# An attention block with bilinear feed-forward on one core: batch 0's keys in float32 on both hardware queues, and the small units of batches 1 to 4 in new slots

## The chip, the cores and the metric

The kernel runs on one core of a Trainium2 chip. The metric is the device time of one execution in microseconds (us). The core has the matrix engine TensorE (PE in the profile; PEld is its loading of the stationary operand), VectorE (DVE), ScalarE (ACT), GpSimd (POOL) and SyncE (SP). Each runs its own instructions in program order and waits for the others through semaphores. Sixteen DMA engines move data between memory (HBM) and the on-chip buffers. Loads can be issued from SyncE and ScalarE (two hardware queues, q1 and q10 in the profile) and from GpSimd (the software queue, q0). In this kernel only the software queue's loads change the type, from float32 to float16.

## What is computed

```python
# q, k, v: (8, 8, 576, 64)   phi: (8, 8, 576, 32)   float32
a = exp(phi - max(phi)); a = a / sum(a)             # over the 32 memories
k_m = einsum('bhsm,bhsd->bhmd', a, k)               # 32 memory keys per head
v_m = einsum('bhsm,bhsd->bhmd', a, v)
scores = matmul(q, k_m.T) / sqrt(64)
attn = softmax(scores)                              # over the 32 memories
attn_out = matmul(attn, v_m)
x = attn_out as (4608 tokens, 512)
out = ((x @ w_a) * (x @ w_b)) @ w_out               # 512 -> 1536 -> 512, float32 out
```

The kernel works batch by batch (0 to 7). It folds v_m into w_a and w_b (vab), so that the two up projections act on the attention weights A directly; their product is kept in ht, and the down projection multiplies ht by w_out.

## The kernel before: the parts that matter here

Every engine's order is the order in which the Python code emits instructions. A schedule in strings says in which order the small units of each batch are emitted and between which up and down matmuls they stand.

Start of the program (cuts marked):

```python
    def load_phi(b):
        phis[b] = inp.tile([P, NHP, NI * M], F32, name="phi_sb")
        (nc.sync if b == 0 else nc.gpsimd).dma_start(out=phis[b], in_=rows(phi, b))
    ...
    ht = consts.tile([P, NFF, 2 * S], F16, name="ht")
    k_f32 = ht[:, 0:2].bitcast(F32)                 # unused at this time, so a float32 landing place
    nc.scalar.dma_start(out=k_f32, in_=rows(k, 0)[:, 0:2])
    nc.scalar.preload_act_table_set("natural_log_exp_and_others")
    load_phi(0)
    halves = [slice(0, 2), slice(2, 4)]
    load_q(0, halves[0])                            # these four on the software queue
    load_k(0, halves[1])
    load_q(0, halves[1])
    load_v(0)
    ...
    nc.vector.memset(kv_sbs[0][:, 2], 1.0 / CS)
    nc.vector.tensor_copy(out=kvs[0][:, 0, 0:2], in_=k_f32)     # float32 to float16
    load_wab(0, 512)
    ...                                             # ones, then the other weights and batch 1
```

The units named in the schedule (g is one half of the heads):

```
exp0 exp1   ScalarE: exponential of phi, per half of the heads
ks0 ks1     TensorE: sums of a*k and of a, 36 matmuls; VectorE: reciprocal and scaling (kvm)
kt0 kt1     TensorE: transposes of kvm; VectorE: copy to kvT
vs, vt      the same for the values; from batch 2 on kv + km + kvt do both together
qt0..qt3    VectorE: 32x32 transposes of q
s0 s1, sc   TensorE: scores (per half; both halves)
e0 e1       ScalarE: exponential of the scores (E)
den0 den1   TensorE: denominators; ScalarE: logarithm (L)
nr0 nr1     ScalarE: R = exp(-L); A = E*R on VectorE (batches 0, 1) or GpSimd (from batch 2)
v0a, x0a .. TensorE: folds of values into weights; ScalarE and VectorE: copy to vab
aN bN       TensorE: up matmuls; ScalarE copies the first, VectorE multiplies into ht
yN          N matmuls of the first four down blocks
fN          N dummy matmuls (the warm tile)
L           loads of a later batch on the software queue
```

The schedule (cut to the strings concerned):

```python
    fill(16)
    chain(0, "exp0 exp1 qt0 qt1 f12 ks0 f4 kt0 f2 ks1 f1 s0 e0 kt1 qt2 qt3 f2 den0 f4 s1 e1 nr0 f8 vs0 vs1 den1 f2 vt0 vt1 nr1 f4")
    chain(0, "v0a x0a f4 a0 a1 v0b x0b f4 b0 b1 ...")
    ...
    chain(1, "exp0 exp1 y9 ks0 y3 kt0 qt0 qt1 y1 y3 ks1 qt2 s0 e0 y6 kt1 qt3 den0 y3 s1 nr0 e1 y4 y2 den1 vs0 vs1 vt0 y1 vt1 nr1 hv0a hx0a hv0b y3 hx0b y2")
    ...
    ups(half_steps(1, 1, 4), slots(2, "- kvt qt3 sc+e0+e1 - den0+den1 nr0+nr1 v0+x0a x0b - v1+x1b x1a"))
    second = "v2_+x2a_+exp0 x2b_ exp1 - kv+km qt0 qt1 kvt qt2+qt3 sc+e0 e1+v0+x0a ..."
```

A slot of the last two strings stands after one pair of up matmuls, and an apostrophe means the batch after. Partial products of the down projection are pulled in between at an even rate, and their sums of tokens (h_sums) run on GpSimd.

Of the kernel before, what the change touches and what calls it, by code (L numbers as in the profile page):

```python
# [8 lines left out]
F32 = mybir.dt.float32  # L9
# [9 lines left out]
def kernel(  # L19
# [11 lines left out]
    nc = tc.nc  # L31
# [38 lines left out]
    def rows(x, b):  # L70
        return x[b].rearrange("h s d -> (h s d)").rearrange("(c p f) -> p c f", c=NHP, p=P)

    phis, qs, kvs = {}, {}, {}
    kv_sbs = [consts.tile([P, 3, NHP, NI * D], F16, name=f"kv_sb{t}") for t in range(2)]

    def load_phi(b):
        phis[b] = inp.tile([P, NHP, NI * M], F32, name="phi_sb")
        (nc.sync if b == 0 else nc.gpsimd).dma_start(out=phis[b], in_=rows(phi, b))

    def load_k(b, hps=slice(0, NHP)):  # L80
        kvs[b] = kv_sbs[b % 2]
        nc.gpsimd.dma_start(out=kvs[b][:, 0, hps], in_=rows(k, b)[:, hps])

    def load_v(b, hps=slice(0, NHP)):
        nc.gpsimd.dma_start(out=kvs[b][:, 1, hps], in_=rows(v, b)[:, hps])

    def load_q(b, hps=slice(0, NHP)):
        if b not in qs:
            qs[b] = inp.tile([P, NHP, NI * D], F16, name="q_sb")
        nc.gpsimd.dma_start(out=qs[b][:, hps], in_=rows(q, b)[:, hps])  # L90

    def load(b):
        load_phi(b)
        load_k(b)
        load_v(b)
        load_q(b)

    def load_wab(lo, hi):
        nc.gpsimd.dma_start(out=wa_sb[:, :, lo:hi], in_=wa_rows[:, :, lo:hi])
        nc.gpsimd.dma_start(out=wb_sb[:, :, lo:hi], in_=wb_rows[:, :, lo:hi])  # L100
# [4 lines left out]


    ht = consts.tile([P, NFF, 2 * S], F16, name="ht")
    k_f32 = ht[:, 0:2].bitcast(F32)
    nc.scalar.dma_start(out=k_f32, in_=rows(k, 0)[:, 0:2])
    nc.scalar.preload_act_table_set("natural_log_exp_and_others")  # L110
    load_phi(0)
    halves = [slice(0, 2), slice(2, 4)]
    load_q(0, halves[0])
    load_k(0, halves[1])
    load_q(0, halves[1])
    load_v(0)
    kvs[0] = kv_sbs[0]

    warm = consts.tile([P, 512], F16, name="warm")
    nc.vector.memset(warm, 0.0)  # L120
# [26 lines left out]
    def fill(n, cols=512):  # L147

        pw = banks.tile([P, 512], F32, name="pw")
        for _ in range(n):  # L150
            nc.tensor.matmul(pw[:, :cols], warm[:, :P], warm[:, :cols], start=True, stop=True)
# [1 line left out]
    ident = consts.tile([P, P], F16, name="ident")  # L153
    make_identity(nc, ident)
    nc.vector.memset(kv_sbs[0][:, 2], 1.0 / CS)
    nc.vector.tensor_copy(out=kvs[0][:, 0, 0:2], in_=k_f32)
    load_wab(0, 512)

    ones = consts.tile([P, 4, 32], F16, name="ones")
# [6 lines left out]
    load_wab(1024, 1536)  # L166
    load_wo(0)
    load_phi(1)
    load_k(1)
    load_q(1, halves[0])  # L170
# [418 lines left out]
    def up_half(b, i, hf, x):  # L589
        ps = banks.tile([P, HALF], F32, name=("pa", "pb")[x])  # L590
        for g in range(2):
            nc.tensor.matmul(ps, vabs[b][x][:, g, P * i:P * (i + 1)], attn[b][:, g, HALF * hf:HALF * (hf + 1)],  # L592
                             start=(g == 0), stop=(g == 1))
        if x == 0:
            if b == 0:
                n = (2 * i + hf) % 20
                a_sbs[b, i, hf] = spare[:, HALF * n:HALF * (n + 1)]
            else:
                a_sbs[b, i, hf] = apool.tile([P, HALF], F16, name="a_sb")
            nc.scalar.copy(out=a_sbs[b, i, hf], in_=ps)  # L600
        else:
            t0 = S * (b % 2) + HALF * hf
            nc.vector.tensor_tensor(out=ht[:, i, t0:t0 + HALF], in0=a_sbs.pop((b, i, hf)), in1=ps, op=ALU.mult)  # L603

    def up(b, i, hfs):
        for hf in hfs:
            up_half(b, i, hf, 0)
        if len(hfs) > 1:
            yield
        for hf in hfs:  # L610
            up_half(b, i, hf, 1)
        yield

    def ups(steps, side=()):

        side = iter(side)
        for step in steps:
            for _ in up(*step):
                work.advance()
                next(side, us[step[0]]["-"])()  # L620
        for f in side:
            work.advance()
            f()
# [5 lines left out]
    def half_steps(b, hf, lo=0):  # L629

        return [(b, i, (hf,)) for i in range(lo, NFF)]
# [10 lines left out]
    def slots(b, names):  # L642

        def both(fs):
            return lambda: [f() for f in fs]
        def unit(n):
            if n == "fin":
                return lambda: work.pull(-work.done % NFF)
            if n == "L":
                return lambda: load(b + 2) if b + 2 < B else None  # L650
            if n[0] == "y":
                return lambda: some(int(n[1:]))
            if n[0] == "d" and n[1:].isdigit():
                return lambda: work.pull(int(n[1:]))
            return us[b + n.endswith("'") - n.endswith("_")][n.rstrip("'_")]

        return [both([unit(n) for n in x.split("+")]) for x in names.split()]
# [3 lines left out]
    def some(n):  # L661
        for _ in range(n):
            next(early, None)

    def chain(b, plan):


        for x in plan.split():
            if x[0] == "f":
                fill(int(x[1:]), 256)  # L670
            elif x[0] == "y":
                some(int(x[1:]))
            elif x[0] in "ab":
                i, _, hf = x[1:].partition(".")
                for h in ([int(hf)] if hf else (0, 1)):
                    up_half(b, int(i), h, "ab".index(x[0]))
            else:
                us[b][x]()
# [3 lines left out]
    chain(0, "v0a x0a f4 a0 a1 v0b x0b f4 b0 b1 a2 b2 v1a x1a a3 b3 a4 a5 v1b x1b a6 a7 b4 b5 v2a x2a b6 b7 a8 a9")  # L682
    load(2)
    chain(0, "v2b x2b a10 a11 b8 b9 b10 b11")
    chain(1, "exp0 exp1 y9 ks0 y3 kt0 qt0 qt1 y1 y3 ks1 qt2 s0 e0 y6 kt1 qt3 den0 y3 s1 nr0 e1 y4 y2 den1 vs0 vs1 vt0 y1 vt1 nr1 hv0a hx0a hv0b y3 hx0b y2")
    load(3)
    sum_weights()
    ups(steps(1, 0, 4), slots(1, "- hv1a+hx1a hv1b+hx1b+y1 - v1a+x1a y3+v1b x1b y3"))
    ups(half_steps(1, 0, 4), slots(1, "- v2a+x2a+v2b+x2b+qt0' - - qt1'+exp0'+qt2' exp1' - kv'+km'+y9"))
    work.plan(S + HALF, 10)  # L690
    ups(half_steps(1, 1, 4), slots(2, "- kvt qt3 sc+e0+e1 - den0+den1 nr0+nr1 v0+x0a x0b - v1+x1b x1a"))
    second = "v2_+x2a_+exp0 x2b_ exp1 - kv+km qt0 qt1 kvt qt2+qt3 sc+e0 e1+v0+x0a den0+x0b v1+x1a nr0+L x1b+exp0' den1 - nr1+v2+x2a - x2b+exp1' - kv'+km' qt0'+qt1' - qt2'+kvt'+qt3'"
    every = "- sc+e0 e1 den0 v0+x0a+x0b - - nr0+exp0' - - v1+x1a qt0' x1b+den1 exp1' - v2+x2a+x2b nr1+qt1' kv'+km' qt2' - qt3' - kvt'+L -"
    last = "sc+e0 - e1 - v0+x0b - x0a den1 - - den0 v1+x1b x1a+nr0 - - - - nr1+v2+x2a - - - - - x2b"
    for b in range(2, B):
# [37 lines left out]
```

The softmax here doesn't subtract the row's maximum and nothing guards it: scores larger than these inputs give would overflow.

## Time and profile before

| what | value |
|---|---|
| median of 3 runs | 245.89 us (245.75 to 246.15) |
| profiled span | 244.0 us, granted TensorE clock 0.996 |
| busy: TensorE, VectorE, ScalarE, GpSimd | 234.6, 166.2, 157.2, 155.6 us |
| read from HBM, written | 42.47 MB, 9.44 MB |
| TensorE busy from 0 to 8 us, 8 to 16, 16 to 24 | 6.74, 6.93, 7.41 us |
| from 32 to 41, 41 to 49, 63 to 74 | 8.05, 7.68, 10.36 us |
| from 230 to 244 | 9.83 us |
| to landing: phi and first keys of batch 0 (hardware queues) | 6.2 and 5.8 us |
| to landing: second keys of batch 0 (software queue) | 7.6 us |

The page's second part cuts the span into 40 slices of 6.1 us, and each digit is the busy share of a slice in tenths. A line of the time line reads: start in us, duration in us, engine, line of the program, operation, output and input tiles, shape, number of instructions merged, and in brackets how long the engine stood idle before and what ended the wait. A line of the waits reads: engine, tile and line, whom it waited for, total us, times, longest. Where several matmuls are merged, the duration runs from the first start to the last end, so that a wait between them is inside it; the end of a matmul is modelled, and those of neighbours overlap.

### The profile page before, as it was taken

How to read it: one execution, taken by the hardware profiler on the slowest of the kernel's cores; microseconds unless marked ns; L12 is line 12 of the kernel's file. 1: busy time of each engine (PE TensorE's matmuls, PEld its weight loads, DVE VectorE, ACT ScalarE, POOL GpSimd, SP SyncE). 2: the span in 40 equal slices, each digit the busy share in tenths (PEclk: the TensorE clock that was granted, in tenths of full speed). 3: DMA queues.
4: the chain of work that ended last, by engine and by line, in shares of the span. 5: the costliest groups of instructions: out<-in, count | busy, mean ns of one | idle time of the engine just before them, and what ended most of it. 6: DMA issues, size and time to landing. Idle time of an engine off the chain costs nothing.

```text
span 244.0 us, 7661 instructions
## 1 busy us (share of the span) xinstructions
PE 234.6 (96%) x3043; PEld 168.1 (69%) x3043; DVE 166.2 (68%) x401; ACT 157.2 (64%) x406; POOL 155.6 (64%) x130
## 2 busy tenths in 40 slices
PE   7989998999989999999999999999999999999993
PEld 2555654456757857767788777877787878888882
DVE  3446773568949968875994659865996676756642
ACT  2265761679598589578956768587856867565330
POOL 8722263499879629892889759892849177937001
PEclk9999999999999999999999999999999999999998
DMA  6999999999937955973159732696120403042154
GB/s 198 211 207 206 209 254 208 254 224 280 224 89 167 205 110 121 236 128 81 41 146 205 177 86 46 166 203 152 34 58 3 89 0 87 3 89 61 42 128 118
DMA packets 25044, 33.82 MB, mean 139 GB/s; under 512 B 1936, under 2 KB 19472, under 8 KB 25008
## 3 DMA queue, kind: packets, MB, share of 16 engines
q0 software_dynamic: 18288, 22.84, 50.8%
q1 hardware_dynamic: 6208, 9.70, 15.8%
q10 hardware_dynamic: 512, 0.79, 1.0%
q8 instruction: 24, 0.39, 0.7%
q14 instruction: 12, 0.10, 0.1%
HBM read 42.47 MB, written 9.44 MB: 213 GB/s over the span
## 4 chain that ended last, share of the span: by engine, by line
PE 76%; DMA 16%; DVE 3%; ACT 2%; issue 1%; POOL 0%; DVEq 0%
PE pa L592 17%; PE py L464 17%; PE pb L592 16%; PE pv L464 8%; DMA wo_sb<-in_moe_w_out_dram 7%; DMA wa_sb<-in_moe_w_a_dram 6%; PE pva L337 5%; PE px L464 4%; PE po L389 3%; DMA ht<-in_k_dram 2%; PE pkv L212 2%; PE pscore L292 1%; PE pD L314 1%; PE pT L241 1%; ACT E L305 1%
## 5 line engine op out<-in xcount | busy, mean ns | idle before, releaser
L603 DVE TENSOR_TENSOR ht<-a_sb,pb 128x288 f16<-128x288 f16 x168 | 73.2, 448 | 39.4 <-ACT a_sb L600 29.9
L592 PEld LDWEIGHTS <-vab 128*128 128x128 f16 x768 | 71.6, 98 | 27.1 <-issue 9.4
L600 ACT CAST a_sb<-pa 128x288 f16<-128x288 f32 x168 | 66.6, 407 | 26.4 <-PE pa L592 24.3
L592 PE MATMUL pa<-A,vab 128*128 128x288 f16 x384 | 75.7, 287 | 0.4 <-DVE vab L349 0.2
L592 PE MATMUL pb<-A,vab 128*128 128x288 f16 x384 | 75.0, 286 | 0.3 <-ACT vab L349 0.3
L446 POOL TENSOR_TENSOR h_sums<-ht 128x768 f16<-128x768 f16 x28 | 45.9, 1642 | 33.0 <-DVE ht L603 32.4
L464 PEld LDWEIGHTS <-h_sums 128*128 128x128 f16 x384 | 37.3, 98 | 7.0 <-issue 0.5
L349 DVE CAST vab<-pva 128x512 f16<-128x512 f32 (+1 forms) x50 | 32.3, 663 | 3.3 <-PE pva L337 2.6
L349 ACT CAST vab<-pva 128x512 f16<-128x512 f32 (+1 forms) x50 | 27.9, 581 | 9.3 <-PE pva L337 9.1
L464 PEld LDWEIGHTS <-ht 128*128 128x128 f16 x288 | 28.1, 98 | 5.7 <-issue 0.4
L464 PE MATMUL py<-w_sums,h_sums 128*128 128x256 f16 x192 | 30.4, 272 | 0.0
L446 POOL TENSOR_TENSOR h_sums<-ht,h_sums 128x768 f16<-128x768 f16 x14 | 23.0, 1642 | 1.0
L446 POOL TENSOR_TENSOR h_sums<-h_sums,ht 128x768 f16<-128x768 f16 x14 | 23.0, 1642 | 0.9
L325 POOL TENSOR_TENSOR A<-E,R 128x576 f16<-128x576 f16 x12 | 15.3, 1278 | 8.8 <-ACT R L323 8.6
L305 ACT ACTIVATE E<-pscore 128x288 f16<-128x288 f32 x32 | 11.4, 417 | 14.5 <-PE pscore L292 14.5
L464 PE MATMUL pv<-w_sums,h_sums 128*128 128x256 f16 x96 | 16.2, 273 | 0.0
L464 PE MATMUL py<-wo_sb,ht 128*128 128x256 f16 x96 | 16.0, 273 | 0.0
L471 ACT ACTIVATE u<-py 128x256 f32<-128x256 f32 x32 | 12.6, 393 | 5.2 <-PE py L464 4.9
L203 DVE STREAM_TRANSPOSE qT<-q_sb 128x288 f32<-128x288 f32 x32 | 14.3, 461 | 2.3 <-DMA q_sb<-in_q_dram 2.3
L464 PE MATMUL py<-w_sums,ht 128*128 128x256 f16 x96 | 15.5, 272 | 0.1
L464 PE MATMUL px<-wo_sb,ht 128*128 128x256 f16 x96 | 15.4, 273 | 0.0
L194 ACT ACTIVATE exp_sb<-phi_sb 128x576 f16<-128x576 f32 x16 | 11.0, 698 | 5.3 <-DMA phi_sb<-in_phi_dram 5.3
(65 smaller groups left out, 274.5 us busy)
## 6 DMA issues: line engine op xcount, KB each, us to landing
out_dram<-o_sb SPq DMA_DIRECT2D x68, 128.0 KB, 2.4
kv_sb<-in_v_dram POOLq DMA_DIRECT2D x7, 576.0 KB, 11.4
phi_sb<-in_phi_dram POOLq DMA_DIRECT2D x7, 576.0 KB, 5.2
kv_sb<-in_k_dram POOLq DMA_DIRECT2D x7, 576.0 KB, 9.0
q_sb<-in_q_dram POOLq DMA_DIRECT2D x6, 576.0 KB, 13.6
wa_sb<-in_moe_w_a_dram POOLq DMA_DIRECT2D x3, 512.0 KB, 14.4
wb_sb<-in_moe_w_b_dram POOLq DMA_DIRECT2D x3, 512.0 KB, 16.2
wo_sb<-in_moe_w_out_dram POOLq DMA_DIRECT2D x3, 512.0 KB, 18.1
```

The lines of the kernel that those rows point to most:

```text
L194: nc.scalar.activation(out=t["exp"][:, 2 * z:2 * z + 2, :, :], in_=phis[b][:, 2 * z:2 * z + 2, :].rearrange("p c (i m) -> p c i m", m=M), ...
L203: nc.vector.transpose(out=t["qT"][:, hp, :].bitcast(F32), in_=qs[b][:, hp, :].bitcast(F32))
L305: nc.scalar.activation(out=Ev[:, g, :, z, :], in_=pss, func=AF.Exp, scale=1.0 / (8.0 * CS))
L325: engine.tensor_tensor(out=attn[b][:, g, sl], in0=t["E"][:, g, sl], in1=t["R", g][:, sl], op=ALU.mult)
L337: nc.tensor.matmul(t["pva", lo, z][g][0][32 * j:32 * j + 32, 0:hi - lo], t["kvT"][64 * r:64 * r + 64, 4 + g, M * j:M * j + M], w_sbs[z][64 ...
L349: engine_copy(out=vabs[b][z][:, g, lo:hi], in_=pva[:, 0:hi - lo])
L446: engine.tensor_tensor(out=out, in0=in0, in1=in1, op=op)
L464: nc.tensor.matmul(po, lhs[:, i], rhs[:, i], start=first and i == 0, stop=i == KH - 1, skip_group_check=not first)
L471: nc.scalar.mul(out=x, in_=po, mul=scale)
L592: nc.tensor.matmul(ps, vabs[b][x][:, g, P * i:P * (i + 1)], attn[b][:, g, HALF * hf:HALF * (hf + 1)], start=(g == 0), stop=(g == 1))
L600: nc.scalar.copy(out=a_sbs[b, i, hf], in_=ps)
L603: nc.vector.tensor_tensor(out=ht[:, i, t0:t0 + HALF], in0=a_sbs.pop((b, i, hf)), in1=ps, op=ALU.mult)
```

## The change

Batch 0's keys arrive in two halves of two head pairs each, both in float32, one on each hardware queue, into space of ht that is free until the first up products; VectorE casts each half. phi of batch 0 goes to the software queue ahead of q and the values. This is to have all of the keys early. The order of the small units of batch 1 and of batches 2 to 4 is new in three strings, to have the inputs of a matmul ready when TensorE comes to it.

The diff without what only moves lines:

```diff
-        (nc.sync if b == 0 else nc.gpsimd).dma_start(out=phis[b], in_=rows(phi, b))
+        nc.gpsimd.dma_start(out=phis[b], in_=rows(phi, b))
 ...
-    k_f32 = ht[:, 0:2].bitcast(F32)
-    nc.scalar.dma_start(out=k_f32, in_=rows(k, 0)[:, 0:2])
+    k_f32 = ht[:, 0:4].bitcast(F32)
+    halves = [slice(0, 2), slice(2, 4)]
+    for engine, x in zip((nc.sync, nc.scalar), halves):
+        engine.dma_start(out=k_f32[:, x], in_=rows(k, 0)[:, x])
     nc.scalar.preload_act_table_set("natural_log_exp_and_others")
     load_phi(0)
-    load_q(0, halves[0])
-    load_k(0, halves[1])
-    load_q(0, halves[1])
+    for x in halves:
+        load_q(0, x)
     load_v(0)
 ...
-    nc.vector.tensor_copy(out=kvs[0][:, 0, 0:2], in_=k_f32)
+    for x in halves:
+        nc.vector.tensor_copy(out=kvs[0][:, 0, x], in_=k_f32[:, x])
 ...
-    chain(1, "exp0 exp1 y9 ks0 y3 kt0 qt0 qt1 y1 y3 ks1 qt2 s0 e0 y6 kt1 qt3 den0 y3 s1 nr0 e1 y4 y2 den1 vs0 vs1 vt0 y1 vt1 nr1 hv0a hx0a hv0b y3 hx0b y2")
+    chain(1, "exp0 y1 exp1 y11 ks0 ks1 y1 qt0 y3 kt0 qt1 s0 e0 kt1 y6 qt2 qt3 den0 y3 s1 nr0 y4 vs0 e1 vs1 den1 y1 vt1 y2 vt0 nr1 hv0a hx0a hv0b y2 hx0b y3")
 ...
-    ups(half_steps(1, 1, 4), slots(2, "- kvt qt3 sc+e0+e1 - den0+den1 nr0+nr1 v0+x0a x0b - v1+x1b x1a"))
-    second = "v2_+x2a_+exp0 x2b_ exp1 - kv+km qt0 qt1 kvt qt2+qt3 sc+e0 e1+v0+x0a den0+x0b v1+x1a nr0+L x1b+exp0' den1 - nr1+v2+x2a - x2b+exp1' - kv'+km' qt0'+qt1' - qt2'+kvt'+qt3'"
+    ups(half_steps(1, 1, 4), slots(2, "qt3 kvt - sc+e0+e1 - den0+den1+nr0 - v0+nr1+x0a x0b - v1+x1b x1a"))
+    second = "v2_+x2a_+exp0 x2b_ exp1 - kv+km qt0 kvt+qt1 - qt2+qt3 sc+e0 e1+v0+x0a den0+x0b nr0+v1+x1a L x1b+exp0' - exp1' v2+x2a den1+qt0' x2b - nr1+qt1'+kv'+km' - - qt2'+kvt'+qt3'"
```

The instructions are the same in kind and number, but for one cast of 128 x 1152 more on VectorE and one load of half the keys that no longer casts. Batch 0's own strings and those of the later batches are as before.

More of the change, by code (lines that the diff above doesn't have):

```diff
@@ L107 @@
     ht = consts.tile([P, NFF, 2 * S], F16, name="ht")
-    k_f32 = ht[:, 0:2].bitcast(F32)
-    nc.scalar.dma_start(out=k_f32, in_=rows(k, 0)[:, 0:2])
+    k_f32 = ht[:, 0:4].bitcast(F32)
+    halves = [slice(0, 2), slice(2, 4)]
+    for engine, x in zip((nc.sync, nc.scalar), halves):
+        engine.dma_start(out=k_f32[:, x], in_=rows(k, 0)[:, x])
     nc.scalar.preload_act_table_set("natural_log_exp_and_others")
     load_phi(0)
-    halves = [slice(0, 2), slice(2, 4)]
-    load_q(0, halves[0])
-    load_k(0, halves[1])
-    load_q(0, halves[1])
+    kvs[0] = kv_sbs[0]
+    for x in halves:
+        load_q(0, x)
     load_v(0)
-    kvs[0] = kv_sbs[0]
     warm = consts.tile([P, 512], F16, name="warm")
```

## The prediction

> **What bounds the kernel now.** I read the page's busy shares first, then the slices, then the waits of TensorE, then the time line where TensorE stood idle.
>
> ```profile
> PE 234.6 (96%) x3043; PEld 168.1 (69%) x3043; DVE 166.2 (68%) x401; ACT 157.2 (64%) x406; POOL 155.6 (64%) x130
> PE   7989998999989999999999999999999999999993
> DMA  6999999999937955973159732696120403042154
> ```
>
> TensorE is busy 234.6 of 244.0 us, so only 9.4 us of idle time exist in the whole span. The stage table puts them so: 4.2 us in the last 14 us (230 to 244), 2.9 us before 24 us, 0.95 us from 32 to 41, 0.32 from 41 to 49, 0.64 from 63 to 74, 0.31 from 74 to 110, almost nothing later. Part of the early "busy" time is dummy matmuls (the warm tile). The change touches nothing after about 104 us, so the 4.2 us tail stays. What can be won is some of the other 5.2 us, and time in which a row of matmuls is stretched by a wait inside it (the page counts that as busy).
>
> The DMA row is full up to about 67 us: to there the order and speed of the loads set when work can begin. The waits of TensorE name it:
>
> ```profile
> PE pk L255 <- DMA kv_sb<-in_v_dram: 0.8, 1, 0.8
> PE pk L255 <- DMA kv_sb<-in_k_dram: 0.8, 1, 0.8
> PE po L389 <- DMA wo_sb<-in_moe_w_out_dram: 0.2, 1, 0.2
> ```
>
> The three are, in time, batch 0's values (15.75 us), batch 1's keys (37.23) and the second third of the output weights (41.10). The last third was issued at 33.1 and took 14.8 us, so it landed at 47.9; the five output matmuls that need it began at 48.01. These landings are gates: lateness ahead of a gate is forgiven as far as TensorE would have waited there.
>
> The start, from the time line of the first 22 us:
>
> ```profile
> 6.67 0.76 DVE L156 CAST kv_sb<-ht 128x1152 f16<-128x1152 f32 x1 [3.06 <-DMA ht<-in_k_dram]
> 7.04 1.26 ACT L194 ACTIVATE exp_sb<-phi_sb 128x576 f16<-128x576 f32 x2 [4.40 <-DMA phi_sb<-in_phi_dram]
> 8.37 0.84 DVE L203 STREAM_TRANSPOSE qT<-q_sb 128x288 f32<-128x288 f32 x2 [0.80 <-DMA q_sb<-in_q_dram]
> 8.81 0.68 PE L255 MATMUL pk<-kv_sb,exp_sb 64*32 64x128 f16 x36
> 15.75 0.78 PE L255 MATMUL pk<-kv_sb,exp_sb 64*32 64x64 f16 x72 [0.84 <-DMA kv_sb<-in_v_dram]
> ```
>
> phi is there at 7.04, the first half of q at 8.37. The first real matmuls start at 8.81 because the 28 dummy ones end at 8.8 (1.26 + 7.62); their inputs were ready at 7.7. Later, four rows of other views matter:
>
> ```profile
> 71.07 2.51 POOL L325 TENSOR_TENSOR A<-E,R 128x576 f16<-128x576 f16 x2 [1.81 <-ACT R L323]
> 66.01 0.72 PE L292 MATMUL pscore<-qT,kvT 32*32 32x288 f16 x32
> 103.54 1.15 PE L292 MATMUL pscore<-qT,kvT 32*32 32x288 f16 x32
> 99.20 1.27 POOL L325 TENSOR_TENSOR A<-E,R 128x576 f16<-128x576 f16 x1
> ```
>
> The attention weights of batch 2 are ready at 71.07 + 2.51 = 73.58 and its first up matmul starts at 73.55 by the modelled ends: GpSimd holds TensorE there. Scores of batches 2 and 4 take 0.72 and 1.15 us, those of batch 3 (at 85.65) 0.47 for the same 32 matmuls: the first two are stretched by 0.25 and 0.68 us.
>
> **What the Trainium skill says.** "DMA: Bandwidth & Descriptors", section "Issuing engines are not separate DMA queues": loads from all queues run on the same 16 DMA engines and interleave. The trace agrees: from 5 to 7 us queues q0, q1 and q10 hold 70%, 29% and 17% of the engines at once. So moving a load between queues changes its place, not the total. "SBUF — State Buffer", section "SBUF: two separate sides": an fp32 copy on VectorE can lock GpSimd out of writing descriptors. The new cast is such an op, but in this trace GpSimd's issues run several loads ahead, so I expect no gap. "VectorE: DVE Perf Modes", section "The perf-mode tier table", has the fp32 copy at twice the base rate; the measured 0.76 us for 1152 elements fits, and I use the measured figure.
>
> **The change part by part.**
>
> 1. *Queues.* phi goes from the first hardware queue to the head of the software queue; the two halves of batch 0's keys have one hardware queue each; the software queue loses the second half of the keys. The same bytes are read, and from q's second half on the software queue has the same order. By the DMA view from 3 to 5 us, phi's queue spent 39.4% of 16 engines on 215 packets (1152 B) and the keys' 55.0% on 187 (2304 B), so 59 and 94 ns each: 512 x 59 / 16 = 1.9 us against 256 x 94 / 16 = 1.5 us of the 16 engines. The hardware queues' load falls from 3.4 to 3.0 us. Software packets begin only near 5.5 us (7 of 314 packets between 4.4 and 5.6), so the hardware queues should be nearly done by then and everything behind may land 0 to 0.4 us earlier. phi, now first on the software queue, lands about where q's first half landed: 8.2 us, 1.2 later. q's first half takes the slot of the second half of the keys, issued at 2.18 with 7.6 us to landing: 9.7 us, 1.4 later.
>
> 2. *Start of batch 0.* Exponentials 8.2 to 9.5 instead of 7.04 to 8.30; the first half is done at 8.9, so the first sums start near 9.1, **+0.3**. VectorE's order is fixed: two casts (+0.76), then the q transposes, then the reciprocal of the first sums. The transposes wait for q until 9.7 and end at 10.6, so the reciprocal goes from 9.54 to about 10.7 and the chain behind it (transpose, scores) is **about 1.1 later**. At 14.9 TensorE used to run out and wait 0.84 for the values. That gate takes most of it: the value sums start near 15.9, +0.15. VectorE's product for A (15.28 before) slips by about 1.1 and lies ahead of the two value scalings, so the first fold starts about 0.4 later, and that runs on to 36 us: **+0.35**.
>
> 3. *Chain of batch 1.* Three output matmuls (3 x 0.22 = 0.65 us) move ahead of the key sums, into the 0.80 us wait. TensorE now reaches the sums at 36.43 + 0.65 + 0.35 = 37.4, about the landing (37.2), and the start's lateness ends here. In exchange no work stands between the key transpose and the scores: PSUM copy 0.30 plus q transpose 0.45 leave it idle about 0.8 us. The other transpose (0.25) moves ahead of the 41.1 gate. Both versions have done that transpose and six output matmuls by 42.7. The same 32 output matmuls precede the 47.9 gate. **At 49.1: 0, within 0.25.**
>
> 4. *Batch 2.* The q transpose moves ahead of kvT's copy, which should remove the stretch of the scores: **-0.2**. One R exponential (0.68) moves ahead of a cast and a partial product, the other stays behind: GpSimd starts A about 0.6 earlier, but its second product now waits for the later R, and ends near 73.3 instead of 73.58: **-0.2**.
>
> 5. *Batches 3 and 4.* Batch 3's kvT transposes move from 82.16 to 81.16, right behind scalings that end at 81.33: **+0.1**. Two q transposes of batch 4 leave the stretch between the scalings (end 101.13) and kvT's copy (102.97): 0.83 us of VectorE work goes to earlier idle time, so kvT is ready by 102.7 and the scores lose most of their delay (they could start at 103.3): **-0.6**. Batch 3's second R moves four places later, and on GpSimd one token sum (1.64) now precedes that A. Its end moves from 100.47 towards 101.4 to 101.8, and the first up matmul of batch 3 was at 101.61: **+0.2**.
>
> Sum: 0 - 0.2 - 0.2 + 0.1 - 0.6 + 0.2 = -0.7. Not all of several small gains adds up on a program with fixed orders, so I take -0.6: 245.89 - 0.6 = **245.3 us**.
>
> **Rivals.** *(a) The late start is not forgiven.* For it: part 2 makes everything from 9 us later, and the gate at 37.2 is already filled with the three moved matmuls. Against it: two more landings, at 41.1 and 47.9, must be waited for by both versions. It would add 0.3 to 0.6: 245.6 to 245.9. *(b) GpSimd becomes the bound at batch 3.* For it: A ends only 1.1 us before it is used now, and a 1.64 us sum is put ahead. If nothing on GpSimd runs earlier, TensorE waits 0.5 us or more and the gain at batch 4 is eaten: about 245.7. Against it: the first A of batch 3 and the loads behind it come one slot earlier, which pulls the queue up. *(c) The loads as a whole finish earlier,* because phi uses the hardware queues poorly (part 1): then the gates at 41.1 and 47.9 come 0.3 to 0.4 earlier, but TensorE can use that only if its own work is done by then. 244.9.
>
> **Range and chances.** The known terms are each below 0.7 us, 0.3% of the time, and all idle time before 110 us is 5.2 us, 2.1%, much of it at the very start. No single term reaches the 4.9 us that 2% would be. I put the low end at all gains plus rival (c), 244.6, and the high end at (a) and (b) together, 246.2. Faster by over 2%: 0.01; within 2%: 0.97; slower by over 2%: 0.02, for a load that is blocked in a way the trace doesn't show.
>
> **What would show it.** Part 1: phi's wait on ScalarE ends at 8.0 to 8.4, q's at 9.5 to 9.9. Part 2: first sums at 9.0 to 9.3, value sums at 15.6 to 16.1. Part 3: no wait for batch 1's keys, a new one of 0.6 to 0.9 us ahead of its first scores, and the first up matmul of batch 1 at 49.1 (it was at 49.10). Part 4: batch 2's scores under 0.55 us. Part 5: batch 4's scores under 0.7 us, and the second A of batch 3 last before its up matmuls. I am wrong if phi lands after 9 us, if batch 1's up matmuls begin beyond 49.6, or if TensorE waits over 0.5 us for A at 101.

## The result, and the profile after

| | before | changed |
|---|---|---|
| median | 245.84 us (245.75 to 246.15) | 243.74 us (243.63 to 243.83) |
| ratio, 95% interval | | 0.9911 [0.9891, 0.993] |
| profiled span | 244.0 us | 241.9 us |

The change takes 2.1 us off, nearly 0.9%. The prediction was 245.3 us with a range from 244.6, so the time lies 0.9 us below the range. Executions of about 258 to 261 us, some 15 us over the others, occurred now and then and are left out throughout.

The page of the changed kernel, its busy shares and the slices that answer to those of before:

```profile
PE 232.9 (96%) x3043; PEld 167.8 (69%) x3043; DVE 167.1 (69%) x402; ACT 157.0 (65%) x406; POOL 155.9 (64%) x130
...
PE   7889999999999999999999999999999999999993
...
DMA  6999999999948938962279632795210303033154
```

Nothing in them says where 2 us went: shares and slices look as before. The busy time of TensorE fell by 1.7 us with the same 3043 matmuls. Part of that are rows with a wait inside them that are shorter now (batch 4's scores, by 0.52 us), and part is the 28 dummies at the start, which took 6.99 us instead of 7.62. The waits of TensorE say more (engine, tile and line, whom it waited for, total us, times, longest):

```profile
PE pk L256 <- issue: 0.7, 1, 0.7
PE pT L274 <- DVE kvm L266: 0.6, 1, 0.6
PE pscore L293 <- DVE kvT L277: 0.4, 1, 0.4
PE pva L338 <- DVE kvT L277: 0.3, 1, 0.3
```

All three waits for a DMA are gone, and what stands in the list instead is short. To find where the time was won, I set the start of the same up matmul in both traces side by side. The difference is changed minus before, in us:

| up matmul | before | changed | difference | gained since the row above |
|---|---|---|---|---|
| first of batch 0 | 18.91 | 18.95 | +0.04 | |
| first of batch 1 | 49.10 | 48.44 | -0.66 | -0.70 |
| first of batch 2 | 73.55 | 72.21 | -1.34 | -0.15 at batch 2's scores, -0.53 behind them |
| first of batch 3 | 101.61 | 100.29 | -1.32 | 0 |
| fifth of batch 3, behind batch 4's scores | 104.63 | 102.58 | -2.05 | -0.72 |
| end of the span | 244.01 | 241.94 | -2.07 | 0 |

So there are three places, and after 104 us nothing changes. The start, from the time line of the changed kernel (start, duration, engine, line, operation, tiles, shape, number, then the idle time and what ended it):

```profile
7.72 1.26 ACT L195 ACTIVATE exp_sb<-phi_sb 128x576 f16<-128x576 f32 x2 [5.10 <-DMA phi_sb<-in_phi_dram]
...
8.46 0.68 PE L256 MATMUL pk<-kv_sb,exp_sb 64*32 64x128 f16 x36 [0.22 <-ACT exp_sb L195]
...
8.97 0.84 DVE L204 STREAM_TRANSPOSE qT<-q_sb 128x288 f32<-128x288 f32 x2 [1.35 <-DMA q_sb<-in_q_dram]
...
15.00 0.58 PE L256 MATMUL pk<-kv_sb,exp_sb 64*32 64x64 f16 x52
16.25 0.33 PE L256 MATMUL pk<-kv_sb,exp_sb 64*32 64x64 f16 x20 [0.67 <-issue]
```

The value sums no longer wait for the values: they start at 15.00 instead of 15.75. But they stop after 52 of 72 matmuls, and the rest comes 0.67 us later. "issue" means that the profile shows no semaphore and no load that was waited for. So a gate at 15.75 was lifted and another stop ends at 16.25, and the start gains nothing.

Batch 1, from TensorE's time line between 34 and 50 us:

```profile
37.06 1.02 PE L256 MATMUL pk<-kv_sb,exp_sb 64*32 64x128 f16 x72
...
39.67 0.82 PE L293 MATMUL pscore<-qT,kvT 32*32 32x288 f16 x16 [0.40 <-DVE kvT L277]
...
47.01 0.30 PE L338 MATMUL pva<-wa_sb,kvT 64*32 64x256 f16 x8 [0.33 <-DVE kvT L277]
...
48.44 0.65 PE L593 MATMUL pa<-A,vab 128*128 128x288 f16 x4
```

Two more rows of the kernel before, and VectorE's second q transpose in the changed one:

```profile
40.41 0.45 PE L292 MATMUL pscore<-qT,kvT 32*32 32x288 f16 x16
...
47.27 0.70 PE L337 MATMUL pva<-wa_sb,kvT 64*32 64x256 f16 x8
```

```profile
39.53 0.47 DVE L204 STREAM_TRANSPOSE qT<-q_sb 128x288 f32<-128x288 f32 x1
```

The new order costs TensorE two waits at the first scores. It stands for 0.40 us ahead of them, until VectorE has copied kvT. Another 0.37 us lie inside their row, which takes 0.82 us instead of 0.45: all but the first two of the 16 matmuls start from 40.06 on, when the second q transpose has ended (39.53 + 0.47 = 40.00). The 0.33 us ahead of the folds are not new. Before, such a wait stood inside the row of the folds, which took 0.70 us for the eight matmuls that take 0.30 here.

The landings are all earlier. GpSimd, which waits for the second third of the output weights before it issues its next load, shows that; first the kernel before, then the changed one:

```profile
41.59 0.74 POOL L90 DMA_DIRECT2D q_sb<-in_q_dram  x1 [1.78 <-DMA wo_sb<-in_moe_w_out_dram]
```

```profile
40.59 0.74 POOL L90 DMA_DIRECT2D q_sb<-in_q_dram  x1 [1.72 <-DMA wo_sb<-in_moe_w_out_dram]
```

The issue that waits for this landing comes 1.00 us earlier. Batches 2 and 4 in the changed kernel (scores of batch 2, GpSimd's second product for A, the first up matmuls of batch 2, scores of batch 4):

```profile
65.35 0.61 PE L293 MATMUL pscore<-qT,kvT 32*32 32x288 f16 x32
...
71.13 1.28 POOL L326 TENSOR_TENSOR A<-E,R 128x576 f16<-128x576 f16 x1 [0.17 <-ACT R L324]
...
72.21 0.53 PE L593 MATMUL pa<-A,vab 128*128 128x288 f16 x2
...
102.01 0.63 PE L293 MATMUL pscore<-qT,kvT 32*32 32x288 f16 x32
```

The scores of batch 2 take 0.61 us (0.72 before), those of batch 4 0.63 (1.15). Before, both products for A ended at 73.58, now at 71.13 + 1.28 = 72.41, 1.17 earlier, of which 0.81 is the lead that the scores already had. But the first up matmul starts at 72.21, 0.20 ahead of that end: it reads only the first product, so something else must have held it at 73.55 before. The second matmul of that row reads the second product. It starts at 72.46, 0.05 us behind the product's end, and stretches the row to 0.53 us, where the kernel before has no stretch:

```profile
73.55 0.41 PE L592 MATMUL pa<-A,vab 128*128 128x288 f16 x2
```

So GpSimd holds TensorE by 0.12 us in the changed kernel. Counted at this second matmul (73.68 before), the gain behind the scores is 0.41 us; another 0.11 comes behind the next folds.

### The profile page after: what moved, and what is told of

Read it like the earlier page. It is cut to its first block, busy times and chain, and to the rows that moved or that the text cites. A ratio compares the mean times of both kernels' runs of the same rounds, so it can differ in the third digit from the quotient of the medians.

```text
span 241.9 us, 7661 instructions
## 1 busy us (share of the span) xinstructions
PE 232.9 (96%) x3043; PEld 167.8 (69%) x3043; DVE 167.1 (69%) x402; ACT 157.0 (65%) x406; POOL 155.9 (64%) x130
## 4 chain that ended last, share of the span: by engine, by line
PE 88%; ACT 3%; DMA 3%; DVE 2%; issue 1%; POOL 0%; DVEq 0%; POOLq 0%
PE pa L593 20%; PE pb L593 19%; PE py L465 17%; PE pv L465 8%; PE pva L338 5%; PE po L390 5%; PE px L465 4%; DMA q_sb<-in_q_dram 3%; PE pkv L213 2%; PE pscore L293 2%; PE pD L315 2%; PE pk L256 1%; ACT E L306 1%; PE pT L242 1%; PE pw L151 1%
## 5 line engine op out<-in xcount | busy, mean ns | idle before, releaser
L204 DVE STREAM_TRANSPOSE qT<-q_sb 128x288 f32<-128x288 f32 x32 | 14.4, 463 | 1.8 <-DMA q_sb<-in_q_dram 1.8
L316 ACT ACTIVATE L<-pD 128x288 f32<-128x288 f32 x32 | 11.4, 424 | 4.7 <-PE pD L315 4.3
## 6 DMA issues: line engine op xcount, KB each, us to landing
q_sb<-in_q_dram POOLq DMA_DIRECT2D x6, 576.0 KB, 13.4
```

Source lines behind the costliest of these rows:

```text
L204: nc.vector.transpose(out=t["qT"][:, hp, :].bitcast(F32), in_=qs[b][:, hp, :].bitcast(F32))
```

## The experiments

### Which part of the change gains: queues, batch 1's order, slots

Each part alone, and the whole without batch 1's new order. In terms of the diff: the first takes the changed kernel with the three old strings, the second the kernel before with the new `chain(1, ...)`, the third the kernel before with the two new `slots` strings, the fourth the changed kernel with the old `chain(1, ...)`.

```diff
 e1_queues     (from the changed kernel)    three new strings -> the three old ones
 e2_chain      (from the kernel before)     old chain(1, ...) -> new
 e3_slots      (from the kernel before)     old slots(2, ...) and second = ... -> new
 e4_no_chain   (from the changed kernel)    new chain(1, ...) -> old
```

> Only the new queues of batch 0's loads; all three strings as before. Theory 'gates': the loads land 1.0 us earlier, and TensorE stood at three of these landings (batch 1's keys, second and third part of the output weights), so the first up matmul of batch 1 moves from 49.10 to about 48.2 and the time falls by 0.7 to 0.9 us to about 245.0. Theory 'order': the 0.66 us won by 49 us came from the new string of batch 1's chain, so this run stays within 0.2 us of 245.84.

> Only the new string of batch 1's chain, old queues, old slots. Theory 'gates': the third part of the output weights still lands at 47.9, so nothing is won, and the two new gaps (ahead of the scores and of the folds) can cost: 245.84 plus 0 to 0.3 us. Theory 'order': 0.66 us faster, 245.2.

> Only the two strings of slots (batch 2's and those of batches 3 and 4), old queues, old chain. If the parts add, this wins what the trace shows after 62 us, 1.4 us: 244.4. If the slots only pay because everything before them is earlier (loads of batch 2 to 4, GpSimd's sums), it wins clearly less, 0.7 us or under.

> The change without the new string of batch 1's chain. Theory 'gates': at least as fast as the whole change, 243.5 to 243.8, since the new chain has two gaps of 0.40 and 0.33 us that the old one doesn't have. Theory 'order': 0.66 us slower than the whole change, 244.4.

The kernel before, run beside these four, had a median of 245.55 us.

| | median us | ratio, 95% interval | first up of batch 1 | first up of batch 2 | behind batch 4's scores |
|---|---|---|---|---|---|
| queues only | 245.25 | 0.9981 [0.9969, 0.9994] | -0.25 | -0.25 | -0.25 |
| order of batch 1 only | 245.78 | 1.0009 [0.9997, 1.0021] | -0.07 | -0.07 | -0.07 |
| slots only | 244.70 | 0.9972 [0.9952, 0.9991] | -0.06 | -0.65 | -1.35 |
| queues and slots | 243.40 | 0.9927 [0.9906, 0.9948] | -0.94 | -1.61 | -2.33 |

The last three columns are starts in the trace against the kernel before (its start minus 49.10, 73.55, 104.63). What follows:

- *The new order of batch 1 gains nothing.* Alone it moves the first up matmul by 0.07 us; taken out of the change, that matmul comes at 48.16 instead of 48.44.
- *The slots gain 0.59 us at batch 2 with the old queues and 0.68 with the new ones, and 0.70 to 0.72 at batch 4 with either.*
- *The queues gain 0.94 at batch 1*, if the start is on time.

In the profiled execution of the queues alone the start was not on time, which is why it shows 0.25. Its time line:

```profile
8.84 0.68 PE L256 MATMUL pk<-kv_sb,exp_sb 64*32 64x128 f16 x36 [1.35 <-ACT exp_sb L195]
...
11.66 1.15 PE L256 MATMUL pk<-kv_sb,exp_sb 64*32 64x128 f16 x36
```

The second row is the same work as the first, 36 matmuls, and takes 1.15 us instead of 0.68. The granted clock in the trace was full from 3.92 us on, half from 10.74 to 14.16, then full again. In this execution the dummies had run through early, TensorE stood idle for 1.35 us, and the half clock came after it. Batch 0's first up matmul was 0.94 us late, and part of that lateness was still there at 49 us. Its executions spread over spans of 243.0 to 243.7 us; the lowest is 0.8 below the 243.8 that the kernel before mostly has, near the 0.94 of the run with queues and slots. So the parts add only where the start is on time. The clock isn't all of it: another execution with the queues alone had a span of 243.6 us and no loss of clock, and no trace of it was kept.

The stop inside the value sums isn't the change's own. The run with the order alone has the queues of before, and its values happened to land earlier (14.4 instead of 15.7); there the stop is as well:

```profile
14.93 0.58 PE L255 MATMUL pk<-kv_sb,exp_sb 64*32 64x64 f16 x52
16.24 0.33 PE L255 MATMUL pk<-kv_sb,exp_sb 64*32 64x64 f16 x20 [0.73 <-issue]
```

Same 52 and 20, same end. So the stop isn't bound to the new queues. In the kernel before, the gate of the values, which opened at 15.75, stands in its place.

### Why the loads land 1 us earlier

My theory after the first four runs: a landing counts the last of the 16 DMA engines, and phi's 512 small packets on a hardware queue leave some engines behind. The trace records a completion by each of 16 engines per load. The completion packets of the software queue's first load (half of q before, phi now) started between 6.87 and 8.04 us before, ten of them by 7.16; in the changed kernel between 6.80 and 7.22. The fastest engine gained 0.07 us, the slowest 0.82. The Trainium skill, "DMA: Bandwidth & Descriptors", section "Why a DMA increments its semaphore by 16 and not by 1", says the same of the semaphore: the engines finish independently and each counts; these records agree. The rival was that the hardware queues simply deliver more bytes before the software queue starts. Two tests, both from the run with queues and slots: phi back on SyncE's hardware queue with both halves of the keys on ScalarE's, and the keys in packets of half the size.

```diff
 e5_three_hw
-    for engine, x in zip((nc.sync, nc.scalar), halves):
+    for engine, x in zip((nc.scalar, nc.scalar), halves):
 ...
-        nc.gpsimd.dma_start(out=phis[b], in_=rows(phi, b))
+        (nc.sync if b == 0 else nc.gpsimd).dma_start(out=phis[b], in_=rows(phi, b))
 e8_small_packets
-        engine.dma_start(out=k_f32[:, x], in_=rows(k, 0)[:, x])
+        for y in (slice(0, NI * D // 2), slice(NI * D // 2, NI * D)):
+            engine.dma_start(out=k_f32[:, x, y], in_=rows(k, 0)[:, x, y])
```

> The change without its new chain string, and with phi back on the first hardware queue; both halves of batch 0's keys on the second one, so that all three loads are on hardware queues. Theory 'uneven engines': a phi that goes through a hardware queue leaves some of the 16 DMA engines 1 us behind, and a landing counts the last engine: the weights land 0.8 to 1.0 us later than with phi on the software queue (GpSimd's wait for the second third of the output weights ends near 41.5 instead of 40.5), first up matmul of batch 1 near 49.0, about 244.3. Theory 'early bytes': the more is loaded before the software queue begins at 5.4 us, the better: landings as early as with the change or earlier, 243.4.

> The change without its new chain string, with each half of the keys loaded by two loads of half the columns, so that the hardware queues move packets of 1152 B as they did for phi, and the same bytes. If the small packets made the engines uneven, their spread at the end of the first software load goes from 0.3-0.4 back towards 1.2 us and everything lands 0.5 to 1 us later, about 244.2. If it was phi itself or its queue, nothing lands later by more than 0.3 us: 243.5.

With three loads on the hardware queues the second third of the output weights landed at 41.1 and the last at 47.9, as before the change. A single execution counts here (245.04 us), and its start was 1.9 us late. Small packets: 243.77 us, 0.9932 [0.9914, 0.995], landings at 40.5 and 47.4, first up matmul of batch 1 at 48.52, so 0.36 behind the run it was made from. One execution carries little, so I repeated that run, exchanged its two queues, and took the run with queues and slots beside them once more:

```diff
 e14_swapped, e15_swapped_again: phi on nc.scalar, both halves of the keys on nc.sync
 e16_three_hw_again: as e5_three_hw
 e17_no_chain_third: as e4_no_chain
```

> The change with the old order of batch 1's small units, phi on ScalarE's hardware queue and both halves of batch 0's keys on SyncE's: the earlier run with three hardware loads, with the two queues exchanged. Theory (phi's small packets on any hardware queue leave the DMA engines uneven): the second third of the output weights lands at 40.8 to 41.1 us as in that run and the first up matmul of batch 1 is at 48.8 to 49.1 us. Rival (it is the queue on which phi went, or two loads on ScalarE's queue): it lands at 40.1 to 40.4 us, first up matmul at 48.2 to 48.5 us.

> The two hardware queues exchanged, as before (phi on ScalarE's, both halves of batch 0's keys on SyncE's), once more, because the profile of the first such run was taken in a disturbed execution. Theory (phi's small packets on any hardware queue leave the DMA engines uneven): the second third of the output weights lands at 40.8 to 41.1 us and, if the start isn't delayed otherwise, the first up matmul of batch 1 is at 48.8 to 49.1 us. Rival (the queue on which phi went): landing at 39.7 to 40.4 us, first up matmul at 48.1 to 48.5 us.

> Phi on SyncE's hardware queue and both halves of batch 0's keys on ScalarE's, once more. Theory (phi on a hardware queue leaves the engines uneven): the second third of the output weights lands at 40.8 to 41.1 us again, 245 us if the start isn't disturbed. Rival (the late landing of the first such run came from its disturbed start): it lands at 39.7 to 40.4 us.

> The change with the old order of batch 1's small units and phi on the software queue, as the reference of this call: the second third of the output weights lands at 39.7 to 40.4 us. If the stop of 0.6 to 1.6 us inside the batch 0 value sums (waiting for nothing that the profile shows) makes the spread between executions, this execution's first up matmul of batch 1 is at 48.2 us with a stop of 0.6 to 0.8 us and at 48.8 us with one of 1.6 us.

The exchanged queues gave 244.31 us (0.9938 [0.9926, 0.9951]) and 244.35 (0.9955 [0.9927, 0.9983]). The first of the two left no trace that can be set beside the others. Three hardware loads again: 245.10, 0.9984 [0.9969, 0.9999]. Queues and slots: 243.81, 0.9922 [0.9899, 0.9944]. The landings in the traces, in us:

| loads of batch 0 | runs | second third of the output weights | last third |
|---|---|---|---|
| as before | before, order only, slots only, and the two single moves below | 40.8 to 41.1 | 47.6 to 47.9 |
| as in the change | the changed kernel twice, queues only, queues and slots three times, more dummies | 39.9 to 40.4 | 47.0 to 47.3 |
| the same, small packets | one run | 40.5 | 47.4 |
| three on hardware queues | the first, the repeated, the exchanged | 41.1, 40.4, 40.5 | 47.9, 47.8, 47.4 |

That the new queues bring the landings forward, by 0.7 us on average and by no less than 0.3 from the latest of one group to the earliest of the other, is shown by twelve traces. More loads on the hardware queues don't bring them further forward, so the rival of more bytes falls.

What moved is the last engine, not the mean. The 16 completions of the second third of the output weights, in us:

| | first engine | mean | last engine, the landing |
|---|---|---|---|
| before | 38.91 | 39.61 | 41.06 |
| changed | 38.82 | 39.29 | 40.06 |

It is so in all of these traces. In the five with the loads of before, the mean lies at 39.5 to 39.7 us and the last at 40.8 to 41.1; in the seven with the new ones at 39.2 to 39.3 and 39.9 to 40.4. The mean gains 0.3 us and the last engine 0.8, because the spread from first to last falls from 2.0 to 2.2 us to 1.1 to 1.6.

What makes the engines uneven is shown in part. For the first load of the software queue the spread was 0.9 to 1.4 us with the loads of before and 0.3 to 0.4 in six of the seven traces with the new ones (1.0 in the seventh). With phi back on SyncE's hardware queue it was 1.1 and 1.2, with phi on ScalarE's 0.6, with small packets of the keys 0.5. So phi's place counts, above all on SyncE's queue. But my theory expected landings at 40.8 or later with phi on either hardware queue, and two of the three came at 40.4 and 40.5. What else acts on the engines in the 30 us between stays open.

That the run with three hardware loads needs 245.1 us all the same is a matter of the start: the second half of the keys, second on its queue, made VectorE's cast wait until 9.87, TensorE stood idle, and the granted clock was half from 12.24 to 15.65 us.

The third run with queues and slots shows most plainly what the earlier landings do. TensorE, without the waits of the new order, runs into the gate of the second third again:

```profile
36.19 0.68 PE L256 MATMUL pk<-kv_sb,exp_sb 64*32 64x128 f16 x36
...
40.09 1.46 PE L390 MATMUL po<-wo_sb,ht 128*128 128x512 f16 x6 [0.27 <-DMA wo_sb<-in_moe_w_out_dram]
...
48.12 0.65 PE L593 MATMUL pa<-A,vab 128*128 128x288 f16 x4
```

The first row had waited 0.80 us for batch 1's keys before, and began at 37.23. Now it begins at 36.19 without a wait. The second is the very gate that stood at 41.10 in the kernel before (0.24 us of waiting). It now opens at 40.09, and the up matmuls follow 0.98 us earlier.

### Which moves in the slots gain

Two single moves, each in the kernel before: R of batch 2 in two slots, and two q transposes of batch 4 earlier.

```diff
 e10_r_split (string of batch 2)
-  sc+e0+e1 - den0+den1 nr0+nr1 v0+x0a x0b
+  sc+e0+e1 - den0+den1+nr0 - v0+nr1+x0a x0b
 e9_q_transposes (end of the string "second")
-  nr1+v2+x2a - x2b+exp1' - kv'+km' qt0'+qt1' - qt2'+kvt'+qt3'
+  nr1+v2+x2a qt0' x2b+exp1' - qt1'+kv'+km' - - qt2'+kvt'+qt3'
```

> The kernel before with one thing changed: two q transposes of batch 4 (VectorE) stand three and one slots earlier, ahead of the scalings. If they are what delayed batch 4's scores, the fifth up matmul group of batch 3 moves from 104.63 to 103.9 and the time falls by 0.7 us to 244.9. If the later R and A of batch 3 (left as before here) had a part in it, the gain is under 0.5.

> The kernel before with only the two exponentials R of batch 2 split: the first one slot earlier, the second one slot later; the q transpose and kvT's copy stay. The whole change won 0.53 to 0.67 us between 69 and 73 us. If the split did that, the first up matmul of batch 2 moves from 73.55 to 73.0 and the time falls by 0.5 us to 245.1. If the earlier q transpose did, this run shows under 0.2 us.

Splitting R: 245.08 us, 0.9978 [0.9963, 0.9992]; the first up matmul of batch 2 goes from -0.23 ahead of the split to -0.77, 0.54 us, as much as the 0.53 in the change. VectorE's copies to vab in this run, and the second product on GpSimd:

```profile
71.46 2.55 DVE L349 CAST vab<-pva 128x512 f16<-128x512 f32 x4
...
71.70 1.28 POOL L325 TENSOR_TENSOR A<-E,R 128x576 f16<-128x576 f16 x1 [0.17 <-ACT R L323]
...
72.79 0.53 PE L592 MATMUL pa<-A,vab 128*128 128x288 f16 x2
```

A ends at 72.98 here. The first up matmul (72.79) doesn't wait for that, the second (73.03) does, as in the change. The two R exponentials, the same copies with the product ahead of them, and the folds that need the space they free, in the kernel before:

```profile
70.19 1.36 ACT L323 ACTIVATE R<-L 128x576 f16<-128x576 f32 x2
...
71.88 0.45 DVE L603 TENSOR_TENSOR ht<-a_sb,pb 128x288 f16<-128x288 f16 x1 [1.25 <-ACT a_sb L600]
72.25 2.52 DVE L349 CAST vab<-pva 128x512 f16<-128x512 f32 x4
...
71.90 0.90 PE L337 MATMUL pva<-wa_sb,kvT 64*32 64x512 f16 x8
...
72.99 0.41 PE L337 MATMUL pva<-wb_sb,kvT 64*32 64x512 f16 x7 [0.19 <-DVE vab L349]
```

Here the copies start 0.79 us later, of which 0.23 is the lead of the other run. Ahead of them VectorE takes an up product of ScalarE's cast a_sb, and that cast stood behind both R exponentials (1.36 us). With R split, it stands behind one. So the folds waited for VectorE, VectorE for ScalarE's cast, and the cast for the second R. Splitting R moved A's end as well, from 73.58 to 72.98, and by these times both were needed: before, A ended only 0.10 us ahead of the second up matmul (73.68), so earlier folds alone could have won no more than that.

The two q transposes: 245.18 us, 0.998 [0.9963, 0.9996]; batch 4's scores in that run:

```profile
103.14 0.91 PE L292 MATMUL pscore<-qT,kvT 32*32 32x288 f16 x32
```

0.91 us stands between 1.15 before and 0.63 in the change, and the up matmul behind gains 0.44 of the 0.72 us. The rest comes from the other moves in that string, which I didn't take apart.

### Does the change without the new order of batch 1 beat it?

```diff
 e12_whole_change: the changed kernel itself
 e13_no_chain_again: as e4_no_chain
 e11_more_dummies (from e4_no_chain)
-  chain(0, "exp0 exp1 qt0 qt1 f12 ks0 ...
+  chain(0, "exp0 exp1 qt0 qt1 f18 ks0 ...
```

> The changed kernel itself, beside the other kernels of this call. Every theory expects 243.7 us, 0.991 to 0.992 of the kernel before, and the first up matmul of batch 1 at 48.4 us in its profile.

> The change with the old order of batch 1's small units, once more. Theory (the new order leaves TensorE idle for 0.40 us ahead of the first scores and 0.33 us ahead of the folds and hides no wait, since the keys now land 1 us earlier): 243.4 us, 0.2 to 0.4 below the whole change, first up matmul of batch 1 at 48.1 to 48.2 us. Rival (the earlier difference was from execution to execution): equal to the whole change within 0.1 us.

> The change with the old order of batch 1's small units and 18 dummy matmuls instead of 12 after batch 0's exponentials. Theory: the dummies keep TensorE busy up to the first sums, so that the granted clock doesn't fall in the executions in which it comes to full early; 243.4 us with a narrower spread than without them. Rival: the dummies delay the first sums where they run at the low clock, by up to 0.4 us, and the wait for the values no longer forgives it: 243.8 us.

| | median us (range) | ratio, 95% interval |
|---|---|---|
| whole change | 243.88 (243.32 to 244.48) | 0.9927 [0.9908, 0.9945] |
| without batch 1's new order | 244.20 (243.40 to 244.81) | 0.9935 [0.9916, 0.9953] |
| the latter, more dummies | 243.49 (243.32 to 244.17) | 0.9918 [0.9903, 0.9932] |

The intervals overlap: none of the three is shown to beat another, and my expectation of 243.4 for the second failed here. The trace of the second shows what blurs it:

```profile
17.07 0.33 PE L256 MATMUL pk<-kv_sb,exp_sb 64*32 64x64 f16 x20 [1.57 <-issue]
```

The stop in batch 0's value sums was 1.57 us this time, and the first up matmul of batch 1 came at 48.80. In the two other executions without the new order the stop was 0.56 and 0.75 us and that matmul at 48.12 and 48.16; with the new order, twice, 0.66 and 0.67 us and 48.44. So at equal stops the new order costs 0.3 us, and from one execution to the next the stop moves the start by more than that. The dummies did as the rival said, too: the first sums came at 9.32 instead of 8.39, but the half clock that they were to prevent didn't occur in either profile, so whether they help stays open.

## Why the prediction was wrong, step by step

| step | predicted us | measured us |
|---|---|---|
| part 1, landings of weights and batch 1's keys | 0 to 0.4 earlier | 0.7 to 1.0 earlier |
| part 2, phi, q | 8.0 to 8.4, 9.5 to 9.9 | 7.72, 8.97 |
| part 2, first sums | 9.0 to 9.3 | 8.46 |
| part 2, start of batch 0's folds | +0.35 | +0.05 (17.84 against 17.79) |
| part 3, TensorE idle at batch 1's scores | 0.6 to 0.9 | 0.40 + 0.37 |
| part 3, first up of batch 1 | 0, within 0.25 | -0.66 |
| part 4, batch 2's scores | -0.2 | -0.15 |
| part 4, A of batch 2 | -0.2 | -0.53 at the first up matmul, -0.41 at the second |
| part 5, batch 3's kvT and second R | +0.1 and +0.2 | 0 |
| part 5, batch 4's scores | -0.6 | -0.72 |

**The step that failed is "At 49.1: 0, within 0.25".** It rested on part 1's "0 to 0.4 us earlier", which came from the packets' time divided evenly by 16 engines. That is the mean of the engines, and the mean did gain 0.32 us at the second third of the output weights. A landing is the last engine, and it gained 1.00. The gates at 37.2, 41.1 and 47.9 were taken as fixed, and all of them moved, by 1.0, 1.0 and 0.7 us. Rival (c) was right in its kind and sized at 0.3 to 0.4. With the old order the gates give 0.94 to 0.98; the new order gives 0.3 of that back. So the part that I took to be neutral costs a little, for just the reason that part 3 gave: "no work stands between the key transpose and the scores". That wait was sized rightly: 0.40 us ahead of the scores and 0.37 inside their row make 0.77. The wait for batch 1's keys, which it was to fill, had gone by itself.

**The start** was predicted to be later by the reciprocal that queues behind the q transposes. That happened, but smaller, as q came 0.7 us sooner than I put it: the reciprocal ran at 9.74 instead of 10.7, against 9.54 before. The first sums even came 0.35 us sooner than before, which is partly luck: the clock was granted in full from 5.44 us in this execution and from 6.72 in that of before, and phi was there at 7.72. The product for A then slipped by 0.16 (15.44 against 15.28), and the second scaling of the values ended at 16.92 against 16.89. That the values' gate opened earlier brought nothing either, because of the stop behind it, which no view of before could show. GpSimd did lose time to the new cast, where the prediction expected no gap: the issue beside the two casts took 1.17 us instead of 0.76. Nothing waited for it; GpSimd stood idle for 0.77 us behind it.

**A of batch 2** had a second bound beside it. A's end was put 0.28 earlier and came 1.17 - 0.81 = 0.36 earlier, nearly right, and in the changed kernel it holds the second up matmul, which gained 0.41. But the first gained 0.53. "GpSimd holds TensorE there" was read from two times that agreed, 73.58 and 73.55, and missed that the folds, behind VectorE's copies, ended at the same moment. They held the first up matmul, and those copies came 0.56 earlier. The row of the folds in TensorE's time line, 0.90 us for 8 matmuls that take 0.41 elsewhere, would have shown it.

**Batch 3** cost nothing. Rival (b) rested on a token sum ahead of the second A. That A ended at 98.58 + 1.27 = 99.85 in the changed kernel, 0.44 us ahead of the first up matmul. The margin of 1.1 us shrank as foreseen, but didn't run out. Rival (a), a late start that isn't forgiven, was seen in the run with the queues alone: 0.94 late at the start and still only 0.25 early at 49 us, where an on-time start gave 0.94.

**Right** were that the stretch of both scores shrinks, though batch 2's still took 0.61 us and not under 0.55, and that nothing moves behind 104 us. Against 245.3, the sum of the failed terms is 0.66 (gates) + 0.33 (batch 2 behind its scores) + 0.3 (batch 3) + 0.07 (both scores) + 0.1 (the discount on the sum) = 1.46 of the 1.56 us missed.

## What to carry to other kernels

Where landings gate the work, ask when the slowest of the DMA engines is done, not when their mean is: here the mean moved by 0.3 us and the landing by 1.0. A gate that is lifted uncovers what stood behind it, so look for the next wait before counting its whole length as gain. A reordering that fills one wait is only as good as that wait is lasting: when another part of the same change removes the wait, the reordering's own cost remains.

## What the runs showed of the hardware that I had not expected

The stop in the value sums goes with an instruction load: in the eleven traces that show a stop, the rest of the sums started 2.25 to 2.44 us after the start of the first 16 KB load on the instruction queue, which itself began anywhere from 13.4 to 14.8 us. That load is a single packet of 0.9 to 1.0 us, and in the changed kernel one of the 16 completions of the next weights came 0.82 us behind the other fifteen (16.59 against 15.77). The kernel before has no stop, but there fifteen completions of the values had come by 14.05 and the last came at 15.71, with an instruction load from 13.65 on. So the gate of the values may have been the same load. That it is the cause wasn't tried, in either case.

The granted clock came to full at different times in executions of nearly the same start, from 3.92 to 6.88 us. In the three traces where it fell again, it stayed full for 6.83 us and half for 3.41 us. The Trainium skill, "TensorE: Matmul & The Clock Gate", section "What's actually happening", gives a window of about 3.4 us and half the rate for the cold state; the 3.41 us agree, and the row of 0.68 us took 1.15 at half clock, 1.7 times as long.
